# Two MLPs behind linear attention: the first MLP's block 0 split out of PSUM in turns 2 to 5, the left outputs moved to the sums' bank, three of its products placed among the last turns

## The chip, the cores and the metric

One core of a Trainium2 chip runs the whole kernel. Its engines are PE (TensorE), DVE (VectorE), ACT (ScalarE), POOL (GpSimd) and SP, which issues most DMAs. The metric is the device time of one execution in microseconds.

## What is computed

```python
def phi(x):
    proj = np.einsum('bhsd,df->bhsf', x, w_phi)
    proj = proj - np.max(np.abs(proj), axis=-1, keepdims=True)
    return np.concatenate([np.exp(proj), np.exp(-proj)], axis=-1)
q_p, k_p = phi(q), phi(k)                       # batch 4, heads 8, seq 576, head_dim 64, 128 features
kv, z = einsum('bhsf,bhsd->bhfd', k_p, v), k_p.sum(axis=2)
x = einsum('bhsf,bhfd->bhsd', q_p, kv) / (einsum('bhsf,bhf->bhs', q_p, z)[..., None] + 1e-06)
x = x.transpose(0, 2, 1, 3).reshape(2304, 512)
h = x @ w_in1;  x = np.maximum(0.01 * h, h) @ w_out1            # first MLP, 512 -> 2048 -> 512
h = x @ w_in2;  x = (h * np.tanh(softplus(h))) @ w_out2          # second MLP
```

## The kernel before

All products are of f32 values that are each split into a high part (`fp32r`, rounded by a copy on ACT) and a low part (value minus high part, a subtraction on DVE, L79 to L81); `three` (L83) makes one product from three matmuls, high by high, low by high and high by low. So each operand costs one ACT copy and one DVE subtraction.

**Attention.** A pair is two heads of one batch, 16 pairs in all (`PAIRS`), four of them per batch. Of the 576 positions, 512 are the main part and 64 the left part; left parts of two pairs are handled together. `attention(n)` (L515) is one turn, and works on five pairs at once: it transposes pair n+2 (`transposes`, PE, then a split), takes the cast of its left queries (`q_left`, DVE L361), projects pair n+1 (`q_proj`, copied by ACT as `qd`; `k_proj` with a guard of two DVE steps, L365 and L366), takes the exponentials of pair n (`k_exp`, `kp` and `lp`, once per sign, L388; `qp`) and its sums (`kv`, PE, into the PSUM tile `kvp`; `kv_copy`), the outputs of pair n-1 (`nd`, PE L448 and L453, into `outs`, two banks) and the normalising (`normalise`, DVE L461 `den` to L464 `xn`; `x_left`, ACT L474) and transposing of pair n-2 (`x_t`). POOL makes the maximum over the features for the queries (L408), two reductions per pair, started by ACT's `qd` copies and used by `q_guard` (DVE L412). `start` does the first projections before turn 0, among them pair 0's and the transposes of pair 1.

`x_t` (L477) transposes `xn` into the bank `xt`, forms the left output with one product against `fold` (L484), whose result lies in the last 64 columns of `outs`, copies that to X (ACT, L485), and returns the copy of the main part to X (ACT, L487), which the turn issues later. X holds the tokens in four chunks of 128 features; the pair's place in its batch is the chunk. The first batch's pairs are 0 to 3.

**Weights.** `conv0` (L93) turns w_in and w_out of the first MLP from their 8-byte form into f32, one unit of 128 x 512 per turn from turn 1 on: DVE L134 and L136 at the turn's head, ACT L150, DVE L159 and L162 at its end. The first ten units are also split, in the following turn (`Conv.split`, ACT L215, DVE L216); the last five are stored.

**First MLP.** Tokens go in blocks; block 0 is the main part of batch 0. `window(0, ...)` (L571) splits one chunk of its input X at the end of each of turns 8 to 11. `moe(g)` (L718) issues the g-th product of w_in (`emit_h`, 12 matmuls into a bank of the ring `a`), the leaky step (`leaky`: ACT L654, DVE L657, ACT L658, DVE L661), and the product of w_out for g-2 (`emit_o`, into four banks of the ring `b`, which is laid over the released banks of the attention). `moe(0)` and `moe(1)` stand at the ends of turns 15 and 16, after the normalising of the pairs 14 and 15; the last `x_t` and then `moe(2)` and the rest follow. From `moe(2)` on, weights of block 0 are made at two units per g.

Each engine runs its instructions in the order in which the program issues them (the schedule is a manual one), and so does each DMA queue.

Of the kernel before, what the change touches and what calls it, by code (L numbers as in the profile page):

```python
# [23 lines left out]
def attention_two_mlps_kernel(  # L24
# [18 lines left out]
    KD = DM // P  # L43
# [207 lines left out]
    with tc.manual_schedule():  # L251
# [105 lines left out]
        def q_left(i):  # L357
            s, l = st[i], lf[i // 2]
            c = P + (i % 2) * LEFT
            for x in "hl":  # L360
                nc.vector.tensor_copy(out=s["q" + x][:, HM:HM + LEFT], in_=l[x][:, c:c + LEFT].bitcast(F32))  # L361
# [17 lines left out]
        def k_proj_left(i):  # L379
            l = lf[i // 2]  # L380
            l["kd"] = ap.tile([P, 2, F], F32, tag="kdl", name="kdl", bufs=1)
            t = bank("a")
            three(t[:, 0:2 * F], l["h"][:, 0:P], l["l"][:, 0:P], wbh, wbl)
            k_guard(t[:, 0:2 * F].rearrange("p (n f) -> p n f", f=F), 2, l["kd"])
# [6 lines left out]
        def q_proj(i, c):  # L391
            s = st[i]
            h, o = divmod(c, 2)
            if "qd" not in s:
                s["qd"] = ap.tile([P, 2, S], F32, tag="qd", name="qd")
                s["qm"] = ap.tile([P, 2, S], F32, tag="qm", name="qm", bufs=1)
            t = bank("a")
            n = HM + (h == o) * LEFT
            c0 = h * (HM + (1 - o) * LEFT)
            d0 = (1 - o) * (HM + h * LEFT)  # L400
            f = slice(o * F, (o + 1) * F)
            three(t[:, 0:n], wbh[:, f], wbl[:, f], s["qh"][:, c0:c0 + n], s["ql"][:, c0:c0 + n])
            nc.scalar.activation(out=s["qd"][:, h, d0:d0 + n], in_=t[:, 0:n], func=AF.Copy)  # L403
            half = s.setdefault("half", set())
            half.add(c)
            if {2 * h, 2 * h + 1} <= half:
                qd, qm = s["qd"][:, h, :], s["qm"][:, h, :]
                nc.gpsimd.partition_all_reduce(qm, qd, P, bass_isa.ReduceOp.absmax)  # L408
# [68 lines left out]
        def x_t(i):  # L477
            s = st[i]
            b, p = divmod(i, NP)
            t = pa.tile([P, 512], F32, tag="xt", name="xt")  # L480
            for j in range(NM):
                nc.tensor.transpose(out=t[:, j * P:(j + 1) * P], in_=s["xn"][:, j].rearrange("p h d -> p (h d)"), identity=ident)
            o = s["nd"][:, 1, MAIN - LEFT:MAIN]
            nc.tensor.matmul(out=o, lhsT=s["xl"].rearrange("p h d -> p (h d)"), rhs=fold, start=True, stop=True)  # L484
            nc.scalar.activation(out=X[:, p, C0 + b * LEFT:C0 + (b + 1) * LEFT], in_=o, func=AF.Copy)  # L485
            st[i] = None
            return lambda: nc.scalar.activation(out=X[:, p, b * MAIN:(b + 1) * MAIN], in_=t, func=AF.Copy)  # L487

        def k_exp(i, a):
# [5 lines left out]
        def start():  # L495

            transposes(0, "k")
            split(wbh, wbl, wbd.rearrange("p a f -> p (a f)"))
            transposes(0, "q")
            k_proj(0, 0)  # L500
            transposes(0, "l")
            q_left(0)
            q_proj(0, 1)
            q_proj(0, 2)
            k_proj(0, 1)
            q_proj(0, 0)
            q_proj(0, 3)
            k_proj_left(0)
            transposes(1, "q", "k")
            q_left(1)  # L510
            q_guard(0)
            load(2)
            conv0.load(1)

        def attention(n):  # L515

            x, o, w, p, t = (i if 0 <= i < PAIRS else None for i in range(n - 2, n + 3))
            x_copy = lambda: None  # L520
            if n + 3 < PAIRS:
                load(n + 3)
            if t is not None and t > 1:
                values(t)
            if n >= CONV0:
                conv0.begin()
                conv0.split()
            if p is not None:
                for c in range(4):
                    q_proj(p, c)  # L530
            if x is not None and n < PAIRS:
                normalise(x)
                x_left(x)
            if p is not None:
                for c in range(2):
                    k_proj(p, c)
                if p % 2 == 0:
                    k_proj_left(p)
            if w is not None:
                k_exp(w, 0)  # L540
            if x is not None:
                x_copy = x_t(x)
            if t is not None:
                transposes(t)
                q_left(t)
            if w is not None:
                k_exp(w, 1)
            x_copy()
            conv0.scale()
            if o is not None:  # L550
                nd(o)
            if p is not None:
                q_guard(p)
            conv0.join()
            if w is not None:
                st[w]["qp"] = [exp(st[w]["qd"], "qp", sg) for sg in (1, -1)]
                for a in range(2):
                    kv(w, a)
                kv_copy(w)
            if p is None:  # L560
                normalise(o)
                x_left(o)
            if p is None:
                moe(n - PAIRS + 1)

        order = [(0, MAIN), (MAIN, MAIN), (C0, B * LEFT)] + [(j * MAIN, MAIN) for j in range(2, B)]
        blocks = [(a, c0, n) for a in range(2) for c0, n in order]
        NB = len(blocks)
        win = {}

        def window(j, chunks=range(KD)):  # L571
            a, c0, n = blocks[j]
            for kk in chunks:
                hi = winp.tile([P, MAIN], F32R, tag="wh", name="wh")[:, 0:n]
                lo = winp.tile([P, MAIN], F32R, tag="wl", name="wl")[:, 0:n]
                split(hi, lo, X[:, kk, c0:c0 + n])
                win.setdefault(j, []).append((hi, lo))


# [138 lines left out]
        def moe(g):  # L718
            for x in [g, g + 1] if g == jump else [g + 1] if g > jump else [g]:
                if x < len(seq):  # L720
                    emit_h(seq[x])
                    if seq[x][1][-1] == M - 1 and seq[x][0] + 1 < NB:
                        window(seq[x][0] + 1)
            if g < len(seq):
                j, ms = seq[g]
                if j <= last1:
                    between = leaky(seq[g])
                    if j == 0 and ms[0] >= HEAD:
                        conv1.step(*between)
                        if not conv1.done():  # L730
                            conv1.step()
                        if conv1.at == len(conv1.units):
                            conv2.load(1)
                    else:
                        for f in between:
                            f()
            if 0 <= g - 2 < len(seq) and seq[g - 2][0] <= last1:
                j, ms = seq[g - 2]
                emit_o(seq[g - 2])
                if ms[-1] == M - 1:  # L740
                    for d in range(KD):
                        finish(j, d)
                if 0 < j < last1:
                    conv2.step()
                    if conv2.done() and not w_st:
                        load_w2(0)
                if j == last1:
                    m = ms[0]
                    split_w2(m, (0, 1) if m < M - 1 else (0,))
                    if m < M - 1:  # L750
                        load_w2(m + 1, (0, 1) if m < M - 2 else (0,))
                    else:
                        load_w2(m, (1,))
                        tail[0] = g + 1
            if g == tail[0]:
                split_w2(M - 1, (1,))
            done = None
            if 0 <= g - 3 < len(seq) and seq[g - 3][0] > last1:
                j, ms = seq[g - 3]
                if seq[g - 3] == seq[-1]:  # L760

                    emit_o(seq[-1], (0, 1))
                    finish(j, 0)
                    finish(j, 1)
                    for d in (2, 3):
                        for it in seq[-2:]:
                            emit_o(it, (d,))
                        finish(j, d)
                elif seq[g - 3] == seq[-2]:
                    emit_o(seq[-2], (0, 1))  # L770
                else:
                    emit_o(seq[g - 3])
                    if ms[-1] == M - 1:
                        done = j
            mish(g, done)

        start()
        for n in range(PAIRS + 1):
            attention(n)
            if 0 <= n - PAIRS // 2 < KD:  # L780
                window(0, (n - PAIRS // 2,))
        x_t(PAIRS - 1)()
        ap.release()
        pa.release()
# [44 lines left out]
```

## Time and profile before

| what | value |
|---|---|
| time, median of 3 runs | 981.86 us (980.54 to 982.08) |
| time of the profiled execution | 982.12 us |
| its span, on the core | 980.0 us |
| PE busy | 957.1 us, 98% |
| DVE, ACT, POOL busy | 715.9, 507.2, 69.0 us |
| chain that ended last | PE 83%, DVE 7%, ACT 7% |

The span is the time on the core from the first instruction to the last; the execution's own time is some 2.1 us longer. The attention takes about the first 190 us of the span, the two MLPs the rest. A time in a row counts from the span's start. In the timeline, a bracket behind an instruction is how long its engine stood idle before it, and what released it.

### The profile page before, as it was taken

What the parts mean: (1) busy time and instruction counts of PE and PEld (TensorE: products, weight loads), DVE (VectorE), ACT (ScalarE), POOL (GpSimd) and SP (SyncE); (2) the same over time, 40 slices, a digit from 0 to 9 for tenths busy, and PEclk for the clock granted to TensorE, in tenths of its full rate; (3) what the DMA queues carried; (4) which work ended last, traced back from release to release, by engine and by line L of the source; (5) the groups of instructions that cost most, each with busy time, mean ns of one, the idle gap of its engine ahead of it and who ended that gap; (6) DMA issues with size and microseconds to landing.
All of it is one profiled execution on the core that took longest, in us unless ns stands there. A gap on an engine that the chain in (4) does not pass through costs nothing.

```text
span 980.0 us, 16741 instructions
## 1 busy us (share of the span) xinstructions
PE 957.1 (98%) x6704; PEld 818.4 (84%) x6704; DVE 715.9 (73%) x1271; ACT 507.2 (52%) x886; POOL 69.0 (7%) x36
## 2 busy tenths in 40 slices
PE   7999889899999999999999999999999999999998
PEld 7999778788888889988888888888888988888886
DVE  7899889389936665765334459878977788778875
ACT  5899879555523333333333456445545455445543
POOL 3443434000000000000000000000000000000000
PEclk9999999999999999999999999999999999999999
DMA  7444543235404444442203310001000100001001
GB/s 200 123 130 136 141 112 108 77 115 161 134 22 143 148 142 148 131 147 100 76 1 112 104 55 11 1 1 43 1 1 1 43 1 23 1 0 43 1 1 43
DMA packets 68205, 72.97 MB, mean 74 GB/s; under 512 B 27168, under 2 KB 52640, under 8 KB 68128
## 3 DMA queue, kind: packets, MB, share of 16 engines
q1 hardware_dynamic: 67392, 71.52, 23.8%
q8 instruction: 52, 0.85, 0.4%
q10 hardware_dynamic: 736, 0.39, 0.1%
q14 instruction: 25, 0.20, 0.1%
HBM read 57.48 MB, written 14.42 MB: 73 GB/s over the span
## 4 chain that ended last, share of the span: by engine, by line
PE 83%; DVE 7%; ACT 7%; issue 1%; DMA 0%; POOL 0%; POOLq 0%; ACTq 0%; DVEq 0%
PE a L84 14%; PE a L85 14%; PE a L86 14%; PE b L86 13%; PE b L85 13%; PE b L84 13%; ACT kp L388 2%; ACT qp L388 1%; DVE wl L216 1%; DVE xn L464 1%; DVE mx L365 1%; PE outs L448 1%; DVE qd L412 1%; DVE kd L366 1%; ACT xleft L474 1%
## 5 line engine op out<-in xcount | busy, mean ns | idle before, releaser
L84 PE MATMUL a<-wh,wh 128*128 128x512 f32 (+1 forms) x640 | 235.7, 368 | 0.0
L86 PE MATMUL a<-wh,wl 128*128 128x512 f32 (+1 forms) x640 | 235.4, 368 | 0.0
L85 PE MATMUL a<-wl,wh 128*128 128x512 f32 (+1 forms) x640 | 235.4, 368 | 0.0
L84 PEld LDWEIGHTS a<-wh,wh 128*128 128x128 f32 x640 | 120.6, 188 | 20.4 <-issue 0.2
L85 PEld LDWEIGHTS a<-wl,wh 128*128 128x128 f32 x640 | 120.7, 189 | 20.3
L86 PEld LDWEIGHTS a<-wh,wl 128*128 128x128 f32 x640 | 120.6, 188 | 19.9
L661 DVE TENSOR_TENSOR gl<-g,gh 128x512 fp32r<-128x512 f32 x72 | 49.8, 692 | 110.2 <-ACT gh L658 110.2
L85 PE MATMUL b<-gl,wh 128*128 128x512 f32 (+1 forms) x320 | 117.7, 368 | 0.0
L84 PE MATMUL b<-gh,wh 128*128 128x512 f32 (+1 forms) x320 | 117.7, 368 | 0.0
L86 PE MATMUL b<-gh,wl 128*128 128x512 f32 (+1 forms) x320 | 117.7, 368 | 0.0
L86 PE MATMUL b<-wh,gl 128*128 128x512 f32 x288 | 112.2, 390 | 0.0
L85 PE MATMUL b<-wl,gh 128*128 128x512 f32 x288 | 112.2, 389 | 0.0
L84 PE MATMUL b<-wh,gh 128*128 128x512 f32 x288 | 112.1, 389 | 0.0
L658 ACT ACTIVATE gh<-g 128x512 fp32r<-128x512 f32 x72 | 45.5, 632 | 116.0 <-PE b L86 110.7
L683 ACT ACTIVATE gh<-u 128x512 fp32r<-128x512 f32 x72 | 45.5, 633 | 70.3 <-PE b L85 63.6
L657 DVE TENSOR_TENSOR g<-g,a 128x512 f32<-128x512 f32 x72 | 49.4, 686 | 41.1 <-ACT g L654 38.4
L408 POOL PARTITION_ALL_REDUCE qm<-qd x32 | 68.8, 2197 | 100.7 <-ACT qd L403 94.0
L710 ACT ACTIVATE r<-e,two 128x512 f32<-128x512 f32 x72 | 51.7, 718 | 36.5 <-DVE e L695 36.5
L84 PEld LDWEIGHTS b<-gh,wh 128*128 128x128 f32 x320 | 60.4, 189 | 10.1
L86 PEld LDWEIGHTS b<-gh,wl 128*128 128x128 f32 x320 | 60.3, 189 | 10.0
L85 PEld LDWEIGHTS b<-gl,wh 128*128 128x128 f32 x320 | 60.3, 188 | 9.9
L679 ACT ACTIVATE e<-a 128x512 f32<-128x512 f32 x72 | 43.0, 597 | 47.8 <-PE a L86 26.8
(116 smaller groups left out, 1638.2 us busy)
## 6 DMA issues: line engine op xcount, KB each, us to landing
stage<-in_moe_w_in_dram SPq DMA_DIRECT2D x32, 512.0 KB, 3.8
stage<-in_moe_w_out_dram SPq DMA_DIRECT2D x32, 512.0 KB, 3.6
scr<-c SPq DMA_DIRECT2D x37, 256.0 KB, 2.0
wstage<-scr SPq DMA_DIRECT2D x32, 256.0 KB, 3.7
qn<-in_q_dram SPq DMA_DIRECT2D x16, 256.0 KB, 4.6
vmain<-in_v_dram SPq DMA_DIRECT2D x32, 128.0 KB, 3.4
kn<-in_k_dram SPq DMA_DIRECT2D x15, 256.0 KB, 4.4
out_dram<-X SPq DMA_DIRECT2D x15, 256.0 KB, 2.1
```

Of the source, the lines that this page charges most:

```text
L84: nc.tensor.matmul(out=o, lhsT=wh_, rhs=xh, start=start, stop=False)
L85: nc.tensor.matmul(out=o, lhsT=wh_, rhs=xl, start=False, stop=False)
L86: nc.tensor.matmul(out=o, lhsT=wl_, rhs=xh, start=False, stop=stop)
L216: return lambda: nc.vector.tensor_tensor(out=lo, in0=src, in1=hi.bitcast(F32), op=ALU.subtract)
L388: nc.scalar.activation(out=e, in_=src, func=AF.Exp, scale=float(sg))
L408: nc.gpsimd.partition_all_reduce(qm, qd, P, bass_isa.ReduceOp.absmax)
L657: nc.vector.tensor_tensor(out=g, in0=g, in1=h, op=ALU.max)
L658: nc.scalar.activation(out=hi, in_=g, func=AF.Copy)
L661: nc.vector.tensor_tensor(out=lo, in0=g, in1=hi.bitcast(F32), op=ALU.subtract)
L679: nc.scalar.activation(out=e0, in_=h0, func=AF.Exp)
L683: nc.scalar.activation(out=hi2, in_=u2, func=AF.Copy)
L710: nc.scalar.activation(out=r0, in_=e0, func=AF.Ln, bias=two)
```

## The change

- `x_t` of the pairs of batch 0 (turns 2 to 5) no longer returns the copy of `xt` to X: it returns `window(0, (p,), t)`, which splits the chunk straight out of the PSUM bank `xt` (ACT high part, DVE low part). The calls of `window(0, ...)` at the ends of turns 8 to 11 are gone.
- The left output's product goes to the last 64 columns of the next pair's `kvp` tile instead of `outs`. That tile holds one bank and is the one that the next `kv` will write.
- In `start`, pair 1's q transposes and its left casts come before the left keys' projection, the k transposes after it. In turn 0, the second exponential of the keys comes before the transposes of pair 2.
- In turn 15 the second exponential comes first, then `moe(0)`, then `x_t`; `moe(1)` comes at the end of turn 15; `emit_h` of the third product comes ahead of the last `x_t`, and `moe` leaves it out.

```diff
--- before.py
+++ after.py
@@ -480,10 +480,13 @@
             t = pa.tile([P, 512], F32, tag="xt", name="xt")
             for j in range(NM):
                 nc.tensor.transpose(out=t[:, j * P:(j + 1) * P], in_=s["xn"][:, j].rearrange("p h d -> p (h d)"), identity=ident)
-            o = s["nd"][:, 1, MAIN - LEFT:MAIN]
+            o = st[min(i + 1, PAIRS - 1)]["kvp"][:, MAIN - LEFT:MAIN]
             nc.tensor.matmul(out=o, lhsT=s["xl"].rearrange("p h d -> p (h d)"), rhs=fold, start=True, stop=True)
             nc.scalar.activation(out=X[:, p, C0 + b * LEFT:C0 + (b + 1) * LEFT], in_=o, func=AF.Copy)
-            st[i] = None
+            if i < PAIRS - 1:
+                st[i] = None
+            if b == 0:
+                return lambda: window(0, (p,), t)
             return lambda: nc.scalar.activation(out=X[:, p, b * MAIN:(b + 1) * MAIN], in_=t, func=AF.Copy)
 
         def k_exp(i, a):
@@ -505,9 +508,10 @@
             k_proj(0, 1)
             q_proj(0, 0)
             q_proj(0, 3)
+            transposes(1, "q")
+            q_left(1)
             k_proj_left(0)
-            transposes(1, "q", "k")
-            q_left(1)
+            transposes(1, "k")
             q_guard(0)
             load(2)
             conv0.load(1)
@@ -538,12 +542,17 @@
                     k_proj_left(p)
             if w is not None:
                 k_exp(w, 0)
+            if n == 0:
+                k_exp(w, 1)
+            if n == PAIRS - 1:
+                k_exp(w, 1)
+                moe(0)
             if x is not None:
                 x_copy = x_t(x)
             if t is not None:
                 transposes(t)
                 q_left(t)
-            if w is not None:
+            if w is not None and 0 < n < PAIRS - 1:
                 k_exp(w, 1)
             x_copy()
             conv0.scale()
@@ -560,20 +569,20 @@
             if p is None:
                 normalise(o)
                 x_left(o)
-            if p is None:
-                moe(n - PAIRS + 1)
+            if n == PAIRS - 1:
+                moe(1)
 
         order = [(0, MAIN), (MAIN, MAIN), (C0, B * LEFT)] + [(j * MAIN, MAIN) for j in range(2, B)]
         blocks = [(a, c0, n) for a in range(2) for c0, n in order]
         NB = len(blocks)
         win = {}
 
-        def window(j, chunks=range(KD)):
+        def window(j, chunks=range(KD), src=None):
             a, c0, n = blocks[j]
             for kk in chunks:
                 hi = winp.tile([P, MAIN], F32R, tag="wh", name="wh")[:, 0:n]
                 lo = winp.tile([P, MAIN], F32R, tag="wl", name="wl")[:, 0:n]
-                split(hi, lo, X[:, kk, c0:c0 + n])
+                split(hi, lo, X[:, kk, c0:c0 + n] if src is None else src)
                 win.setdefault(j, []).append((hi, lo))
 
 
@@ -718,7 +727,8 @@
         def moe(g):
             for x in [g, g + 1] if g == jump else [g + 1] if g > jump else [g]:
                 if x < len(seq):
-                    emit_h(seq[x])
+                    if x != HEAD:
+                        emit_h(seq[x])
                     if seq[x][1][-1] == M - 1 and seq[x][0] + 1 < NB:
                         window(seq[x][0] + 1)
             if g < len(seq):
@@ -777,8 +787,7 @@
         start()
         for n in range(PAIRS + 1):
             attention(n)
-            if 0 <= n - PAIRS // 2 < KD:
-                window(0, (n - PAIRS // 2,))
+        emit_h(seq[HEAD])
         x_t(PAIRS - 1)()
         ap.release()
         pa.release()
```

In `start`, on DVE, around the casts of pair 1's left queries (`qth`, `qtl` from `lh`, `ll`); `kd` is pair 0's guard, `mx` and `kdl` that of the left keys:

```order
 L366 TENSOR_TENSOR kd<-a,mx 128x512
+L81 TENSOR_TENSOR qtl<-a,qth 128x2x256
+L361 CAST qth<-lh 128x64
+L361 CAST qtl<-ll 128x64
 L365 TENSOR_REDUCE mx<-a 128x2
 L366 TENSOR_TENSOR kdl<-a,mx 128x256
-L81 TENSOR_TENSOR qtl<-a,qth 128x2x256
-L81 TENSOR_TENSOR ktl<-a,kth 128x512
-L361 CAST qth<-lh 128x64
-L361 CAST qtl<-ll 128x64
+L81 TENSOR_TENSOR ktl<-a,kth 128x512
```

The q subtraction and both casts stand ahead of the left keys' guard now, and the k subtraction behind it.

On DVE in turn 2, between the casts of pair 4 and `q_guard` (L412); `wl` is the low part of block 0's first chunk:

```order
 L361 CAST qth<-lh 128x64
 L361 CAST qtl<-ll 128x64
+L81 TENSOR_TENSOR wl<-xt,wh 128x512
 L412 TENSOR_TENSOR qd<-qd,qm 128x1152
 L159 SCALAR_TENSOR_TENSOR e<-stage 128x512
```

The subtraction that read X at the end of turn 8 reads the bank `xt` here; the same is found in turns 3, 4 and 5, and the four of turns 8 to 11 are gone.

On PE in turns 14 and 15, from the sums of pair 14 (`kvp` from `vmain`, `kp`) to the first product of the first MLP (`a` from `wh`):

```order
 L425 MATMUL kvp<-vmain_104,kp 64x65 x16
 L428 MATMUL kvp<-vleft_107,lp 64x2x65 x2
-L482 MATMUL xt<-ident,xn 128x128 x4
-L484 MATMUL outs<-fold,xleft_86 128x64
-L448 MATMUL outs<-kv,qp 64x65 x32
-L453 MATMUL outs<-kv,qp 64x65 x4
-L425 MATMUL kvp<-vmain_102,kp 64x65 x16
-L428 MATMUL kvp<-vleft_105,lp 64x2x65 x2
-L425 MATMUL kvp<-vmain_102,kp 64x65 x16
-L428 MATMUL kvp<-vleft_105,lp 64x2x65 x2
 L84 MATMUL a<-wh,wh_597 128x512
 L85 MATMUL a<-wl,wh_597 128x512
```

The first MLP's product follows the sums of pair 14 at once; the transposes of pair 13, the outputs of pair 14 and the sums of pair 15 come after its twelve matmuls.

## Rows read from the trace of the kernel before

**Rows 1.** Page, first part: busy time, share of the span, instructions, by engine

```profile
PE 957.1 (98%) x6704; PEld 818.4 (84%) x6704; DVE 715.9 (73%) x1271; ACT 507.2 (52%) x886; POOL 69.0 (7%) x36
```

**Rows 2.** Windows: busy us (instructions) of each engine, granted clock, DMA share, GB/s

```profile
178.00:180.00 2.00, 2.00 (x43) 2.00 (x42) 0.69 (x1) 0.40 (x1) 0.00 (x0) 0.50 0.02 7
200.00:220.00 20.00, 20.00 (x90) 16.56 (x89) 19.12 (x36) 10.96 (x20) 0.00 (x0) 1.00 0.39 130
```

**Rows 3.** Timeline of DVE, start; start us, us, instruction, idle before and its releaser

```profile
14.02 0.88 DVE L361 CAST qth<-lh 128x64 fp32r<-128x64 f32 x1
14.82 0.18 DVE L361 CAST qtl<-ll 128x64 fp32r<-128x64 f32 x1
15.78 1.36 DVE L412 TENSOR_TENSOR qd<-qd,qm 128x1152 f32<-128x1152 f32 x1 [0.78 <-POOL qm L408]
18.66 0.69 DVE L365 TENSOR_REDUCE mx<-a 128x4 f32<-128x512 f32 x1 [1.52 <-PE a L86]
...
23.05 1.35 DVE L412 TENSOR_TENSOR qd<-qd,qm 128x1152 f32<-128x1152 f32 x1
...
26.94 0.69 DVE L365 TENSOR_REDUCE mx<-a 128x4 f32<-128x512 f32 x1 [1.87 <-PE a L86]
```

**Rows 4.** Timeline of PE, start

```profile
15.05 0.38 PE L84 MATMUL a<-qth,wbh 128*128 128x320 f32 x1 [2.51 <-DVE qtl L361]
...
23.01 1.16 PE L425 MATMUL kvp<-vmain,kp 128*64 128x65 f32 x32 [0.79 <-ACT kp L388]
...
24.32 0.41 PE L84 MATMUL a<-qth,wbh 128*128 128x320 f32 x1
```

**Rows 5.** Timeline of POOL, two reductions in a row of it

```profile
11.44 4.31 POOL L408 PARTITION_ALL_REDUCE qm<-qd  x2 [11.01 <-ACT qd L403]
...
66.91 4.26 POOL L408 PARTITION_ALL_REDUCE qm<-qd  x2 [6.23 <-ACT qd L403]
...
108.28 4.31 POOL L408 PARTITION_ALL_REDUCE qm<-qd  x2 [6.74 <-ACT qd L403]
```

**Rows 6.** Timeline of DVE, turns 6 to 12

```profile
76.80 0.16 DVE L461 TENSOR_SCALAR den<-outs 128x10 f32<-128x10 f32 x1
...
97.23 0.16 DVE L461 TENSOR_SCALAR den<-outs 128x10 f32<-128x10 f32 x1
...
107.10 0.69 DVE L81 TENSOR_TENSOR wl<-X,wh 128x512 fp32r<-128x512 f32 x1 [1.43 <-ACT wh L80]
...
108.38 1.78 DVE L216 TENSOR_TENSOR wl<-c,wh 128x512 fp32r<-128x512 f32 x1
...
146.30 0.16 DVE L461 TENSOR_SCALAR den<-outs 128x10 f32<-128x10 f32 x1
```

**Rows 7.** Timeline of all engines, end of turn 4

```profile
62.07 1.35 DVE L412 TENSOR_TENSOR qd<-qd,qm 128x1152 f32<-128x1152 f32 x1
62.18 0.62 ACT L487 ACTIVATE X<-xt 128x512 f32<-128x512 f32 x1
...
66.25 0.69 DVE L216 TENSOR_TENSOR wl<-c,wh 128x512 fp32r<-128x512 f32 x1 [0.75 <-ACT wh L215]
```

**Rows 8.** Timeline of PE, turns 14 to 16

```profile
168.68 2.09 PE L448 MATMUL outs<-kv,qp 128*64 128x65 f32 x64 [0.73 <-ACT X L485]
...
174.59 0.63 PE L482 MATMUL xt<-ident,xn 128*128 128x128 f32 x4 [1.27 <-DVE xn L464]
...
176.50 3.66 PE L448 MATMUL outs<-kv,qp 128*64 128x65 f32 x64 [0.90 <-ACT X L485]
...
187.85 2.09 PE L448 MATMUL outs<-kv,qp 128*64 128x65 f32 x64 [1.57 <-ACT X L485]
```

**Rows 9.** Timeline of ACT, turns 15 and 16

```profile
177.29 0.59 ACT L487 ACTIVATE X<-xt 128x512 f32<-128x512 f32 x1
...
185.70 0.60 ACT L654 ACTIVATE g<-a 128x512 f32<-128x512 f32 x1 [1.99 <-PE a L86]
...
187.59 0.20 ACT L485 ACTIVATE X<-outs 128x64 f32<-128x64 f32 x1
```

## The prediction

> **What bounds the kernel now.** I read three views, in this order. The page's first part [rows 1] shows PE busy 957.1 of 980.0 us, so only some 23 us of the span can be had without taking matmuls away. The windows [rows 2] say where: in 200 to 220 us, as in all the MLP stretches after it, PE is busy 20.00 of 20.00 at a granted clock of 1.00, while DVE is busy 19.12; in 178 to 180 it is also always busy, but at a granted clock of 0.50, the lower of its two levels (1.2 GHz). So the losses lie ahead of the MLPs, in the attention turns and their ends. The timelines tell what ends each wait: at the start PE waits for DVE and ACT [rows 3, 4]; in the sixteen turns DVE and ACT hand the work to each other and PE merely follows [rows 6, 7]; in the last turns PE waits again, for copies of ACT and for DVE [rows 8]. From PE's first product of the first MLP after the attention, all that follows is a fixed length of PE work. What the change is worth is therefore how much earlier PE gets there. Three places count.
>
> **Turns: the split taken out of turns 8 to 11.** A turn's head on DVE is the `den` row. From 76.80 to 97.23 are two plain turns (6 and 7): 20.43 us. From 97.23 to 146.30 are turns 8 to 11, each ending with `window`: 49.07 us [rows 6]. Four plain turns would be 40.86; turn 11 has no weight split behind it (L216, 0.69 in [rows 7]), so 40.2. The split of X costs 8.9 us there. The rows show why it costs more than its own 0.69: DVE waits 1.43 us for ACT's high half, and the weight split that follows takes 1.78 instead of 0.69, because it now starts at 108.38, just after POOL's reduction of 108.28 [rows 5, 6], where in a plain turn it is through when POOL starts (66.25 and 0.69 in [rows 7], POOL at 66.91 in [rows 5]). So 1.1 us of each is DVE held up by POOL.
>
> In turns 2 to 5 the same split comes back cheaper. ACT pays nothing: its copy of `xt` into X (0.62 [rows 7]) becomes the high half of the same size, and nothing reads X there before the MLP overwrites it. DVE gets one subtraction of 0.69 more. It stands ahead of `q_guard` and waits for ACT: in an even turn ACT's copy ends at 62.18 + 0.62 = 62.80, DVE was free at 62.07, so 0.73 of waiting and 0.69 of work, 1.42 in all; of this 0.75 was idle before L216 anyway [rows 7], which leaves 0.67. In an odd turn I count no such idle time and ACT's copy as done: 0.69. Four turns: 2.7 us. L216 moves later by 0.7, and so do ACT's `qd` copies that start POOL, so it stays ahead of POOL. Bounds: 4.2 (even turns pay all 1.42) and 1.4 (only odd turns pay). Net gain 8.9 - 2.7 = 6.2, between 8.2 - 4.2 = 4.0 and 8.9 - 1.4 = 7.5.
>
> **Start.** PE stands 2.51 us at 15.05 for the cast of pair 1's left queries, and the casts took 0.88 and 0.18 [rows 3, 4], the first one held up by POOL. The change puts the q transposes three matmuls earlier and the casts right behind the q subtraction; by ACT's 0.60 and DVE's 0.69 the casts run near 13.3, between the holds of POOL's two reductions (11.44 and 2.15 later [rows 5], 1.1 each as above). PE goes on some 1.6 us earlier. The next gate is `q_guard(0)` at 15.78, which waits for POOL and doesn't move; with its 1.36, of which some 0.1 overlaps the next, the guard of pair 1's keys starts at 17.05 and not at 18.66 after 1.52 idle [rows 3]. From there to the end of the casts DVE takes 23.05 - 18.66 = 4.39 [rows 3], to 21.44. In the present order PE starts pair 2's q products only at 24.32, behind the second half of the sums, which waited 0.79 for ACT's second exponential [rows 4]; in the new order both exponentials come before ACT's copies, so PE follows DVE at about 21.5. That is 2.8 earlier, and the guard of pair 2, at 26.94 after 1.87 idle for PE [rows 3], moves with it. I take 2.8. Bounds: 0.8 (only that 0.79 goes, the casts fall into a hold again) and 3.4 (both DVE waits, 1.52 + 1.87). The k transposes move behind the left keys; their DVE subtraction then ends near 14.9, when PE is still at pair 1's q products, so I cost it at nothing. DMA: nothing is added, and SP's issues keep their order.
>
> **Last turns.** PE waits 0.73 (168.68), 1.27 (174.59), 0.90 (176.50) and 1.57 (187.85): 4.47; three of these are `nd` waiting for ACT's copy out of `outs`, one is `x_t` waiting for `xn` [rows 8]. And `nd` takes 3.66 at 176.50 for a usual 2.09, at the lower granted clock [rows 2, 8]: 1.57 more. Together 6.0. With the left product in the `kvp` bank `nd` no longer waits for that copy; with 12 first-MLP matmuls ahead of `x_t(13)`, `x_t(14)` and `x_t(15)`, DVE's `xn` and ACT's scaling are covered each time. PE's idle stretch ahead of 176.5 is filled, so I take the clock to stay up. Two waits are new. First, `kv(15)` writes the `kvp` bank that ACT must first have read (L485), and ACT now has the first MLP's two steps ahead of that read: they would start at 177.29, and from L654 to L485 it is 187.59 - 185.70 = 1.89, so the read ends at 177.29 + 1.89 + 0.20 = 179.4 [rows 9]. PE, without the 0.73, 1.27 and 0.90 but with 2.8 of products, would be through `nd(14)` at about 178.2: a wait of 1.2; behind it in PE's queue stand all the rest. Second, the output banks of the MLP reuse the attention's banks, and the first product into them waits for ACT's last copies; the products that covered this now come before `x_t(15)`, so PE waits for copies of 0.20 and 0.59 [rows 9] and their start, 0.9. Gain 6.0 - 2.1 = 3.9. Bounds: 6.0 (neither wait) and 2.3 (both, and the low clock as now).
>
> Elsewhere, in turns 6 to 14, the new bank does nothing: PE's `nd` starts a little earlier, but PE is not what the turn waits for.
>
> **The sum.** 2.8 + 6.2 + 3.9 = 12.9. The profiled execution took 982.12 us (span 980.0 and 2.1 around it), 0.26 above the median 981.86 of the runs; 982.1 - 12.9 = 969.2. By the bounds, one term at a time, 967.1 to 971.4. The case around the sum has a chance of 0.60. A measurement of this kernel can tell about 0.2% (2 us) from no change.
>
> **Rivals.** *The start keeps its pace*: the casts fall into POOL's hold, or the clock drops as PE's idle times shift. For it: the margin of the casts to the second hold is some 0.3 us. Start 0.8, so 971.2; chance 0.15.
> *The last turns only trade waits*: `kv(15)` waits, and the clock falls in that gap as it did before 178. Against it: single gaps of 1.27 in [rows 8] came together with 0.90 before the fall. Tail 2.3, so 970.8; chance 0.12.
> *The weight split meets POOL in turns 3 to 6*: the moved split pushes L216 behind POOL's start, as it did after turn 8. 4 x 1.1 = 4.4 more, 973.6. Against it: whatever delays L216 also delays the `qd` copies that start POOL; the margin is POOL's start at 66.91 against L216's at 66.25. Chance 0.07. The rows show DVE held for 1.1 us of a reduction of about 2.15 [rows 5, 6]. The Trainium skill (SBUF — State Buffer, Who interferes with whom) states that the two engines share a port pair as an exclusive lock, and that whoever comes second is blocked for the other's whole instruction. By that rule a collision would cost up to about 2.1 us and this rival 975 or more (an estimate); the trace disagrees on the length, and the measured 1.1 decides.
> *Slower*: the shared `kvp` bank ties PE to ACT in every turn. `kv` of turns 2 to 15 may only start when ACT has read the left product of the same turn. The copy ended at about 168.66, and `nd` of 2.09 lies between [rows 8]; with `nd` starting 0.73 earlier the slack is 1.4. If ACT's copy came later than this by d in each of 14 turns, PE's next products, ACT's `qd` copies and POOL would follow: 14 d. It overtakes the 12.9 from d = 0.92; at d = 1.1 it costs 15.4, so 984.6. Against it: the copy's place in ACT's order is unchanged. Chance 0.04. That the gains cancel within 2 us has 0.02.
>
> **How the numbers follow.** Faster holds the first four cases, 0.94. The forecast is the sum's case, 969.2. The range takes in the first three (0.87): its top is 971.2 with 0.8 for the spread of runs (980.54 to 982.08) and 0.5 for small misses in the other terms, 972.5; its low end is 967.3, where start and turns both reach their upper bounds (0.6 + 1.3 less), with 0.8 for that spread and 0.5 as above, 966.0.
>
> **What would show it.** Right: DVE `wl<-xt` in four early turns, turns 2 to 5 about 0.7 longer, turns 8 to 11 like 6 and 7 with every L216 near 0.69; pair 2's q products on PE near 21.5; no PE wait for `xn` in the last turns, one of about 1 us before `kv(15)` and one before the first `b` product. Wrong: L216 rows of 1.8 in turns 3 to 6; the early DVE waits for PE unchanged; a stretch at granted clock 0.50 near 180; or PE waits appearing after 200 us, where DVE is nearly full [rows 2].

## The result and the profile after

The changed kernel took 967.82 us (median of 4 runs, 967.59 to 968.7), the kernel before 981.2 us beside it (4 runs, 980.42 to 982.08): ratio 0.9865, interval 0.9848 to 0.9882, so 13.4 us less. Measured once more at the end, it took 968.77 against 981.15 (ratio 0.987, 0.9856 to 0.9884), 12.4 us less. The forecast was 969.2, with 966.0 to 972.5.

Its profiled execution took 967.76 us, with a span of 965.9. This table cuts both spans at the same instructions: POOL's first reduction, the `den` rows on DVE that head the turns, and PE's first product into the banks `b`. Each length is the difference of two starts. The stretch from the head of turn 15 to the first `b` product is called the tail below.

| stretch | before | after | gain | forecast |
|---|---|---|---|---|
| up to POOL's first reduction | 11.44 | 10.66 | 0.78 | none |
| from there to the head of turn 2 | 24.49 | 21.81 | 2.68 | 2.8 |
| turns 2 to 5 | 40.87 | 43.33 | -2.46 | -2.7 |
| turns 6 and 7 | 20.43 | 20.44 | 0 | 0 |
| turns 8 to 11 | 49.07 | 40.18 | 8.89 | 8.9 |
| turns 12 to 14 | 27.00 | 27.02 | 0 | 0 |
| head of turn 15 to the first `b` product | 23.08 | 18.75 | 4.33 | 3.9 |
| from there to the end of the span | 783.6 | 783.7 | -0.1 | 0 |

**Busy time.** The page's first part, against [rows 1]:

```profile
PE 950.6 (98%) x6704; PEld 813.9 (84%) x6704; DVE 711.6 (74%) x1271; ACT 505.2 (52%) x882; POOL 68.5 (7%) x36
```

ACT has 4 instructions fewer: the four copies of `xt` to X became the high halves, and the four high halves of turns 8 to 11 are gone. PE's matmuls are the same in number. The windows of the last turns and of the MLP, against [rows 2]:

```profile
175.00:180.00 5.00, 5.00 (x88) 4.47 (x87) 2.46 (x5) 2.44 (x6) 0.00 (x0) 1.00 0.53 188
200.00:220.00 20.00, 20.00 (x90) 16.57 (x89) 19.08 (x35) 10.59 (x19) 0.00 (x0) 1.00 0.52 155
```

The stretch at 0.50 is gone, and the MLP is as full as it was.

**Start.** The timeline of DVE, against [rows 3]:

```profile
12.29 0.56 DVE L361 CAST qth<-lh 128x64 fp32r<-128x64 f32 x1
12.39 0.49 DVE L361 CAST qtl<-ll 128x64 fp32r<-128x64 f32 x1
...
14.96 1.36 DVE L412 TENSOR_TENSOR qd<-qd,qm 128x1152 f32<-128x1152 f32 x1 [0.99 <-POOL qm L408]
16.24 0.68 DVE L365 TENSOR_REDUCE mx<-a 128x4 f32<-128x512 f32 x1
...
20.79 1.36 DVE L412 TENSOR_TENSOR qd<-qd,qm 128x1152 f32<-128x1152 f32 x1
...
23.55 0.69 DVE L365 TENSOR_REDUCE mx<-a 128x4 f32<-128x512 f32 x1 [0.72 <-PE a L86]
```

The casts are through at 12.88, as POOL's second reduction begins (10.66 + 2.13 = 12.79), the guard of pair 1's keys (16.24) follows `q_guard(0)` without its 1.52 of idle time, and that of pair 2 waits 0.72 instead of 1.87.

**Turns.** The timeline of all engines in turn 4, against [rows 7] and POOL's 66.91 in [rows 5], and then that of DVE at the heads of turns 6, 8 and 12, against [rows 6]:

```profile
60.60 0.69 DVE L81 TENSOR_TENSOR wl<-xt,wh 128x512 fp32r<-128x512 f32 x1 [0.67 <-ACT wh L80]
61.21 1.35 DVE L412 TENSOR_TENSOR qd<-qd,qm 128x1152 f32<-128x1152 f32 x1
...
64.65 0.69 DVE L216 TENSOR_TENSOR wl<-c,wh 128x512 fp32r<-128x512 f32 x1
...
65.31 2.14 POOL L408 PARTITION_ALL_REDUCE qm<-qd  x1 [6.86 <-ACT qd L403]
```

```profile
75.80 0.16 DVE L461 TENSOR_SCALAR den<-outs 128x10 f32<-128x10 f32 x1
...
96.24 0.16 DVE L461 TENSOR_SCALAR den<-outs 128x10 f32<-128x10 f32 x1
...
136.42 0.16 DVE L461 TENSOR_SCALAR den<-outs 128x10 f32<-128x10 f32 x1
```

DVE's new subtraction waits 0.67 for ACT in an even turn; the weight split (L216) lost its 0.75 of idle time and starts 0.66 before POOL, as it did before (66.25 and 66.91).

**Last turns.** The timeline of PE, against [rows 8], and that of ACT in turn 15, against [rows 9]:

```profile
166.12 2.09 PE L448 MATMUL outs<-kv,qp 128*64 128x65 f32 x64
...
169.46 1.15 PE L425 MATMUL kvp<-vmain,kp 128*64 128x65 f32 x32 [1.02 <-ACT X L485]
...
174.80 0.60 PE L482 MATMUL xt<-ident,xn 128*128 128x128 f32 x4
...
175.49 2.09 PE L448 MATMUL outs<-kv,qp 128*64 128x65 f32 x64
...
182.19 0.50 PE L84 MATMUL b<-gh,wh 128*128 128x512 f32 x1 [0.80 <-ACT X L490]
```

```profile
167.31 0.60 ACT L663 ACTIVATE g<-a 128x512 f32<-128x512 f32 x1
168.66 0.63 ACT L667 ACTIVATE gh<-g 128x512 fp32r<-128x512 f32 x1 [0.76 <-DVE g L666]
169.20 0.21 ACT L485 ACTIVATE X<-kvp 128x64 f32<-128x64 f32 x1
```

`nd` and `x_t` start with no wait and at the upper clock. `kv(15)` waits for ACT's read of the left product, which stands behind two steps of the first MLP on ACT.

### The profile page after: what moved, and what is told of

Same layout as the page of the kernel before. It is cut to its first block, busy times and chain, and to the rows that moved or that the text cites. A ratio compares the mean times of both kernels' runs of the same rounds, so it can differ in the third digit from the quotient of the medians.

```text
span 965.9 us, 16740 instructions
## 1 busy us (share of the span) xinstructions
PE 950.6 (98%) x6704; PEld 813.9 (84%) x6704; DVE 711.6 (74%) x1271; ACT 505.2 (52%) x882; POOL 68.5 (7%) x36
## 4 chain that ended last, share of the span: by engine, by line
PE 85%; DVE 9%; ACT 5%; POOL 1%; issue 1%; DMA 0%; POOLq 0%; ACTq 0%; DVEq 0%
PE a L84 14%; PE a L85 14%; PE a L86 14%; PE b L84 14%; PE b L86 14%; PE b L85 14%; DVE qd L412 1%; DVE mx L365 1%; ACT kp L388 1%; DVE kd L366 1%; DVE xn L464 1%; POOL qm L408 1%; ACT qp L388 1%; DVE wl L216 1%; PE outs L448 1%; PE kvp L425 1%
```

## The experiments

The table has the stretches of the profiles, cut as above, and the medians. The kernel before took 981.02 us beside the first four experiments, 981.33 beside the next four and 981.15 beside the last four. Turns 6 and 7 take 20.43 to 20.45 and turns 12 to 14 27.00 to 27.02 in every profile.

| kernel | POOL first | to turn 2 | turns 2 to 5 | turns 8 to 11 | turn 15 to `b` | median (lowest to highest) |
|---|---|---|---|---|---|---|
| before | 11.44 | 24.49 | 40.87 | 49.07 | 23.08 | 981.2 |
| after | 10.66 | 21.81 | 43.33 | 40.18 | 18.75 | 967.82 |
| e_turns | 12.23 | 23.89 | 43.32 | 40.14 | 21.49 | 974.65 (973.32 to 975.35) |
| e_start | 10.65 | 21.79 | 40.88 | 49.76 | 21.49 | 978.76 (977.36 to 979.66) |
| e_kvp | 11.47 | 24.47 | 40.88 | 49.06 | 18.88 | 978.87 (976.77 to 980.64) |
| e_tail | 11.77 | 23.25 | 40.88 | 49.09 | 18.73 | 978.36 (976.65 to 979.44) |
| e_outs | 11.69 | 21.78 | 43.32 | 40.16 | 24.05 | 974.1 (974.07 to 974.54) |
| e_place | 11.47 | 24.47 | 40.87 | 45.19 | 23.08 | 977.75 (975.89 to 978.25) |
| e_lo | 10.68 | 23.80 | 42.05 | 40.16 | 18.74 | 968.25 (966.4 to 968.81) |
| e_last | 10.64 | 21.77 | 43.35 | 40.16 | 16.80 | 966.71 (965.93 to 967.3) |
| after_again | 11.20 | 21.78 | 43.33 | 40.15 | 18.76 | 968.77 (967.71 to 969.61) |
| e_casts | 12.08 | 21.77 | 43.31 | 40.14 | 18.74 | 968.52 (967.86 to 969.22) |
| e_both | 11.33 | 21.78 | 42.07 | 40.15 | 16.80 | 965.94 (964.73 to 966.49) |
| e_best | 10.56 | 21.83 | 42.05 | 40.15 | 16.81 | 965.64 (964.64 to 966.17) |

**One part of the change alone** (edits to the kernel before; the diffs are pieces of the change's). `e_turns` has the split out of `xt` and no `window(0, ...)` in turns 8 to 11:

> Only the split of block 0 is moved to turns 2 to 5; start, left outputs and last turns as before. Theory (three gains that add up): turns 2 to 5 each about 0.6 us longer than before's 10.5 and 9.9, turns 8 to 11 together 40.2 instead of 49.07, all L216 rows near 0.69; net 6.4 us less, about 975 where before takes 981. The waits of the last turns stay (0.73, 1.27, 0.90, 1.57) with the stretch at granted clock 0.50. Rival (the gain needs the earlier start or the shared bank): L216 still meets POOL in turns 3 to 6 or the gain stays under 4 us.

Ratio 0.9938 (0.992 to 0.9956). Turns 2 to 5 pay 2.45 and turns 8 to 11 save 8.93, as in the whole change. `e_start` has the new order in `start` and turn 0:

> Only the order in the start and in turn 0 is changed. Theory: q_guard of pair 2 (31.85 before) comes 2.7 us earlier relative to POOL's first reduction (11.44 before), and the whole 2.7 us earlier. Rival (what was seen at the start was the first microseconds of another execution): relative to POOL's first reduction under 1 us is left, and the time is as before.

Ratio 0.9978 (0.9967 to 0.9988). The start is 2.70 shorter, as in the whole change. (Its turn 10 ran partly at a granted clock of 0.50, and turns 8 to 11 took 0.7 longer than before's.) `e_kvp` has the left product in the `kvp` bank:

> Only the left outputs move to the kvp bank. Theory: the three waits of nd for ACT's copy go; x_t(13) still waits for xn, so the 0.73 of turn 14 is lost to that wait; 0.90 + 1.57 and perhaps 0.2 stay as gain: 2.5 to 2.9 us if the stretch at granted clock 0.50 stays, 4.1 to 4.5 if it goes. The turns up to 13 keep their heads to 0.1 us. Rival (the last turns gain by the products that fill them): under 1 us, as other waits take the place.

Ratio 0.998 (0.9968 to 0.9991). `e_tail` adds the early first-MLP products to that:

> The left outputs in the kvp bank and the three first-MLP products among the last turns; start and split of block 0 as before. Theory: heads of turns 2 to 14 as before, then 4.3 us gained up to the first product of w_out: waits of about 1.0 before kv(15) and 0.8 before that product, none for xn, no stretch at granted clock 0.50 near 176 to 180. Rival (the clock stays up only because the whole is shifted): the stretch at 0.50 remains and the gain is about 2.7.

Ratio 0.9976 (0.9966 to 0.9986). With the bank alone the profile's tail is 4.20 shorter, and the products add 0.15. In `e_kvp` PE's timeline has one wait left, larger than before:

```profile
174.63 0.63 PE L482 MATMUL xt<-ident,xn 128*128 128x128 f32 x4 [2.09 <-DVE xn L464]
```

The products fill this 2.09 and pay with two new waits, 1.02 and 0.80 in the changed kernel: 0.27 of net gain, of which 0.15 shows. And a caution: `e_turns` and `e_start` leave the last turns as they were, with the same waits, and yet their tail is 1.59 shorter than before's, because the low clock, expected to stay in `e_turns`, did not come (in `e_place`, with the same last turns again, it did: 23.08). PE's timeline of `e_turns`, at the place of 176.50 in [rows 8]:

```profile
168.33 0.63 PE L482 MATMUL xt<-ident,xn 128*128 128x128 f32 x4 [1.26 <-DVE xn L464]
...
170.25 2.09 PE L448 MATMUL outs<-kv,qp 128*64 128x65 f32 x64 [0.89 <-ACT X L485]
```

Waits of 1.26 and 0.89 here, of 1.27 and 0.90 before, and 2.09 against 3.66 for the same matmuls. So of the tail's 4.33 about 1.6 belongs to a fall of the clock that the tail's waits alone do not decide.

The mean granted clock, which is on record for every run beside the experiments and every run of the changed kernels, says how often stretches at the low clock came. The kernel before ran 41 times beside the experiments: 35 times at 0.996 to 0.998, in 980.26 to 983.18 us, and six times at 0.999, in 978.27 to 979.62. The changed kernel had 0.999 or 1.000 in all of its eight runs. With one part of the change alone the mean was 0.998 or less in 3 of 4 runs of `e_turns`, in all ten of `e_start` and of `e_kvp`, and in 8 of 10 of `e_tail`. So the whole change kept the clock up each time, and no part alone did so; where in an unprofiled run the clock was low, and which parts it takes to keep it up, is not shown. Against before's six runs at 0.999 (median 979.5) the changed kernel's eight (median 968.2) are 11.3 us faster.

**The bank undone in the whole change** (`e_outs`).

```diff
-            o = st[min(i + 1, PAIRS - 1)]["kvp"][:, MAIN - LEFT:MAIN]
+            o = s["nd"][:, 1, MAIN - LEFT:MAIN]
```

> The changed kernel with one part undone: the left product goes back into the bank of the main sums (outs); the early split, the start and the early first-MLP products stay. Theory (the two parts of the tail need each other: nd waits for ACT's copy out of outs, and with the first MLP's ACT steps ahead of that copy it waits longer): PE's wait for kvp (1.0) goes, PE's waits for outs come back, about 0.7 in turn 14, about 3 before nd(14) and about 1.6 before nd(15); first b product 3 to 4 us later than in the changed kernel's profile (182.19), so 971 to 972 us. Rival (the early products alone cover the waits, the bank is worth nothing): first b product within 1 us of the changed kernel's, 967 to 969 us. Heads of turns 2 to 12 as in the changed kernel under both, but for the start's own 1 to 2 us.

The ratio to before is 0.9927 (0.9912 to 0.9942): 5.3 to 6.3 us slower than the two measurements of the changed kernel. The tail is 5.30 longer. PE's timeline, and the window behind the largest wait:

```profile
159.77 2.09 PE L448 MATMUL outs<-kv,qp 128*64 128x65 f32 x64 [0.73 <-ACT X L485]
...
170.40 3.61 PE L448 MATMUL outs<-kv,qp 128*64 128x65 f32 x64 [2.44 <-ACT X L485]
...
181.75 2.09 PE L448 MATMUL outs<-kv,qp 128*64 128x65 f32 x64 [1.57 <-ACT X L485]
```

```profile
172.00:174.00 2.00, 2.00 (x42) 2.00 (x40) 0.36 (x1) 0.00 (x0) 0.00 (x0) 0.50 0.41 135
```

0.73 + 2.44 + 1.57 = 4.74 of waits, 1.52 at the low clock (3.61 against 2.09), less the 1.02 for `kvp` that is gone: 5.24. The waits came where the theory had them; its 3 to 4 us were too small by the clock. Without the bank the early products are a loss: 24.05 against before's 23.08, both with a stretch at the low clock. That stretch followed a wait of 2.44 here, and all four runs had a mean granted clock of 0.998.

**The split left late, but put elsewhere in the turn** (`e_place`, an edit to the kernel before).

```diff
             x_copy()
+            if 0 <= n - PAIRS // 2 < KD:
+                window(0, (n - PAIRS // 2,))
             conv0.scale()
...
             attention(n)
-            if 0 <= n - PAIRS // 2 < KD:
-                window(0, (n - PAIRS // 2,))
```

> The kernel before with one edit: the split of X in turns 8 to 11 stays there and still reads X in SBUF, but is written ahead of conv0.scale, nd and q_guard instead of at the turn's end. Theory (the price of the late split is its place: DVE waits 1.4 us for ACT there, and the weight split behind it meets POOL): no L216 of 1.8 us, turns 8 to 11 take 43 to 44.5 us from head to head instead of 49.07, time 976 to 977 us, most of what moving the split to turns 2 to 5 gives (974.65 us). Rival (it needs the read from PSUM in place of ACT's copy, because ACT then has one more instruction of 0.6 in these turns): turns 8 to 11 take 47 us or more, time 979 us or more.

Ratio 0.9957 (0.994 to 0.9973). The timelines of ACT and of DVE in turn 8:

```profile
103.05 0.62 ACT L487 ACTIVATE X<-xt 128x512 f32<-128x512 f32 x1
103.53 0.66 ACT L80 ACTIVATE wh<-X 128x512 fp32r<-128x512 f32 x1
```

```profile
104.22 0.69 DVE L81 TENSOR_TENSOR wl<-X,wh 128x512 fp32r<-128x512 f32 x1 [1.19 <-ACT wh L80]
...
108.28 0.69 DVE L216 TENSOR_TENSOR wl<-c,wh 128x512 fp32r<-128x512 f32 x1
```

No L216 is held by POOL any more, and 3.88 of the 8.89 comes from the place alone. The rest, 45.19 against 40.18, stays: 1.15, 0.81, 1.15 and 1.91 over the plain turns 8 to 11. In turn 8 the rows say what it is: ACT's high half stands behind its copy of `xt` to X, so DVE waits 1.19 for it and then works 0.6, while the 0.75 of idle time that L216 has in a plain turn is gone, 1.05 in all. That is the rival's additional ACT instruction. Turn 11 ends with no L216, and there POOL catches another DVE step (L136, 1.52 instead of 0.42), in this kernel as before. The truth lies between theory and rival: neither's range has 45.19, or the median of 977.75.

**The low part behind the guard** (`e_lo`, an edit to the changed kernel: in turns 2 to 5 the subtraction is issued after `q_guard`).

```diff
             if p is not None:
                 q_guard(p)
+            for lo, src, hi in late:
+                nc.vector.tensor_tensor(out=lo, in0=src, in1=hi.bitcast(F32), op=ALU.subtract)
+            late.clear()
```

> The changed kernel with DVE's low part of the early split (turns 2 to 5) issued behind q_guard instead of ahead of it; ACT's high part stays. Theory (the 0.67 us that DVE waits for ACT in each even turn is on the path, the guard can run in it): turns 2 to 5 cost about 0.6 to 1.4 us together over plain ones instead of 2.45, time 0.8 to 1.4 us under the changed kernel's 967.8, so 966.4 to 967.0; L216 stays at 0.69. Rival (something else ends the turn, as q_guard then waits for PE, or the weight split now meets POOL): turns 2 to 5 within 0.4 of the changed kernel's or longer by up to 4.4, time 967.4 to 972.

Ratio 0.9863 (0.9848 to 0.9878). Turns 2 to 5 are 1.28 shorter, the subtraction never waits, as expected; but the median did not move, as under the rival. What its profiled execution lost lies in the start, which this edit does not touch. PE, then DVE:

```profile
10.76 0.63 PE L341 MATMUL a<-ident,qn 128*128 128x128 f32 x4 [0.21 <-DMA qn<-in_q_dram]
```

```profile
12.10 0.69 DVE L81 TENSOR_TENSOR qtl<-a,qth 128x512 fp32r<-128x512 f32 x1 [1.22 <-ACT qth L80]
12.71 0.18 DVE L361 CAST qth<-lh 128x64 fp32r<-128x64 f32 x1
12.81 1.33 DVE L361 CAST qtl<-ll 128x64 fp32r<-128x64 f32 x1
...
18.41 0.69 DVE L365 TENSOR_REDUCE mx<-a 128x4 f32<-128x512 f32 x1 [1.61 <-PE a L86]
```

PE's transposes of pair 1's queries waited for their load and started 0.39 us later than in the changed kernel's profile (10.37); the second cast met POOL's second reduction (10.68 + 2.13 = 12.81) and took 1.33, and PE went on at a granted clock of 0.50 between 16 and 18 us. The head of turn 2 came 23.80 behind POOL's first reduction instead of 21.8. That is the prediction's rival "the start keeps its pace", in one execution, the run of 968.81 with a mean granted clock of 0.998. The other three had 0.999 or 1.000 and took 966.4, 967.95 and 968.56; why two of them gained nothing is not shown.

**The two new waits in the last turns** (`e_last`, an edit to the changed kernel).

```diff
             if n == PAIRS - 1:
                 k_exp(w, 1)
-                moe(0)
+                emit_h(seq[0])
             if x is not None:
                 x_copy = x_t(x)
+            if n == PAIRS - 1:
+                moe(0)
...
-        emit_h(seq[HEAD])
-        x_t(PAIRS - 1)()
+        emit_h(seq[HEAD], range(KD - 1))
+        x_last = x_t(PAIRS - 1)
+        emit_h(seq[HEAD], (KD - 1,))
+        x_last()
```

> The changed kernel with two edits in the last turns: in turn 15 ACT's copy of the left product comes ahead of the first MLP's first ACT steps, and of the last first-MLP product the fourth chunk comes behind the last x_t instead of ahead of it. Theory (kv(15) waits 1.02 for ACT's read of the kvp bank because two ACT steps of the MLP stand ahead of it, and the first b product waits 0.80 because its cover has gone ahead): both waits fall, the first to 0 and the second to 0.2 or less; first b product 1.3 to 1.7 us earlier, time 966.1 to 966.5. Rival (the waits only hide others, x_t then waits for xn or the first b product for the leaky steps): first b product within 0.4 us of the changed kernel's, 967.4 to 968.2.

Ratio 0.985 (0.9835 to 0.9865); the tail is 1.95 shorter, more than expected (the median, 966.71, is 0.2 above the expected range), and PE's timeline has no wait in it, down to the first `b` product:

```profile
168.22 1.10 PE L425 MATMUL kvp<-vmain,kp 128*64 128x65 f32 x32
...
180.18 0.50 PE L84 MATMUL b<-gh,wh 128*128 128x512 f32 x1
```

Both waits were on the path, with their whole 1.82.

**The casts ahead of the transposes, and all together.** `e_casts` puts the casts of pair 1's left queries ahead of its q transposes; `after_again` is the changed kernel; `e_both` is `e_lo` with `e_last`; `e_best` adds the casts' new place.

```diff
+            parts_of(1, "q", HM + LEFT)
+            q_left(1)
             transposes(1, "q")
-            q_left(1)
```

> The changed kernel itself once more, beside the next three on the same chip. Theory (the start hangs on whether pair 1's left casts get through before POOL's second reduction, which differs between executions): median 967.5 to 968.5; in the profile the head of turn 2 comes either 21.8 us behind POOL's first reduction, with casts of 0.5, or 23.8, with a cast of 1.3. Rival (the late start seen once belongs to another cause, as a late load): some other row ahead of the casts is longer.

> The changed kernel with one edit in the start: the casts of pair 1's left queries come ahead of its q transposes and of the subtraction that waits for ACT, not behind them. Theory (the casts' place is a margin of some 0.3 us before POOL's second reduction): the casts take 0.2 each and end before POOL's second reduction starts, no cast of over 0.5; head of turn 2 at 21.3 to 21.9 us behind POOL's first reduction in every profile; median 0 to 1 us under the changed kernel's of the same call, and a narrower spread. Rival (the casts write the tile that PE still reads for pair 0, so they wait and hold back the q subtraction): head of turn 2 more than 22.2 us behind, median 0.3 or more above.

> The changed kernel with the low parts of the early split behind q_guard (measured alone: turns 2 to 5 1.28 us shorter) and the two edits in the last turns (measured alone: first b product 2.0 us earlier). Theory (they lie in different places and add): 3.3 us under the changed kernel of the same call, less 1 to 2 in executions whose start is late: 964.3 to 966. Rival (they share ACT or the clock, or the weight split of a later turn moves): less than 2 us under it.

> The kernel before this one with the start's casts ahead of the q transposes too: three edits to the changed kernel. Theory: as the last, and its start never late: 3.3 to 4.3 us under the changed kernel of the same call, 963.8 to 965, with a narrower spread. Rival (the casts hold back the q subtraction): no better than the last, 964.3 to 966.

`after_again` showed the first of its two expected starts, 21.78 with casts of 0.56 and 0.50; its median lies 0.3 above the range given for it. `e_casts` was no better (968.52 and 968.77, with spreads of 1.4 and 1.9). The expectation that the casts would take 0.2 fell: they now meet POOL's first reduction. DVE and POOL in `e_best`:

```profile
10.68 1.23 DVE L369 CAST qth<-lh 128x64 fp32r<-128x64 f32 x1
11.82 0.18 DVE L369 CAST qtl<-ll 128x64 fp32r<-128x64 f32 x1
```

```profile
10.56 4.31 POOL L416 PARTITION_ALL_REDUCE qm<-qd  x2 [10.13 <-ACT qd L411]
```

It costs nothing, since `q_guard(0)` still waits for POOL (0.92 in `e_best`, 0.86 in `e_casts`): the head of turn 2 comes 21.83 and 21.77 behind POOL's first reduction, as where the casts pass between the reductions. So 21.8 is set by POOL, and the late start of `e_lo` was not met in these two profiles. Whether the new place removes it can't be told from one profile each. `e_both` is 2.83 under `after_again` in the medians, with 3.2 in the stretches (1.26 in the turns, 1.96 in the tail): they add. `e_best`, 965.64 us, ratio 0.9838 (0.9824 to 0.9851), has the lowest median here, but not measurably under `e_both`: the theory's 963.8 to 965 was missed, and its rival's range holds it.

## Why the prediction was right

*Turns.* 8.89 for 8.9 and 2.46 for 2.7. The working held step by step: the 0.67 of waiting in even turns (0.73 forecast), about 0.6 more in each turn, L216 ahead of POOL with no idle time left before it, and all 32 `wl<-c,wh` rows between 682 and 695 ns. In `e_place` 1.2 went with the place of the late split in each of turns 8, 9 and 10, near the 1.1 at which the prediction priced POOL's hold; in turn 11, where the hold stayed with another step in it, only 0.2.

*Start.* 2.68 for 2.8. With the 0.78 by which POOL began earlier taken off, the rows lie where the sum put them: the guard of pair 1's keys at 16.24 + 0.78 = 17.02 (17.05), PE's q products of pair 2 at 20.95 + 0.78 = 21.73 (21.5). But part of this is luck. `e_tail` and `e_turns`, which have the old start, needed 23.25 and 23.89 and not 24.49, at a granted clock of 1.00 where before had 0.55 and 0.60 in 16 to 20 us. The windows of before and of `e_tail`, and DVE's casts in `e_turns`:

```profile
16.00:18.00 2.00, 2.00 (x12) 2.00 (x11) 1.14 (x1) 1.51 (x5) 0.69 (x1) 0.55 1.04 369
```

```profile
16.00:18.00 2.00, 2.00 (x18) 2.00 (x17) 1.39 (x2) 1.85 (x6) 0.43 (x2) 1.00 1.06 389
```

```profile
14.81 0.88 DVE L361 CAST qth<-lh 128x64 fp32r<-128x64 f32 x1
15.61 0.92 DVE L361 CAST qtl<-ll 128x64 fp32r<-128x64 f32 x1
```

DVE's wait for PE ahead of the guard of pair 1's keys, 1.52 before, was 0.50 in `e_tail` and 1.18 in `e_turns`. In `e_turns` POOL held both casts, in `e_tail` and before only the first. So against executions without that low clock the new order is worth 1.5 to 2.1, and 2.7 against one with it.

*Tail.* 4.33 for 3.9, with both new waits near their forecast: 1.02 for 1.2 and 0.80 for 0.9. (By the prediction's own terms, 176.50 - 2.90 + 2.8 + 2.09, PE would have arrived at 178.5 and not 178.2, and the first wait would be 0.9.) The waits went as it said: no `nd` waits for ACT, and no `x_t` for `xn`. What it did not see is how little the 12 matmuls ahead of each `x_t` add: run alone, the bank gives nearly the whole gain, and the products give back in new waits what they cover. The 1.57 of low clock was counted as the change's because PE's idle stretch is filled. That reason is not shown: the stretch also vanished in `e_turns` and `e_start`, where the tail's waits stayed. The count itself held, with a mean granted clock of 0.999 or more in all eight runs of the changed kernel.

*The rivals.* "The last turns only trade waits" was right on the waits of the products and wrong on the sum. "L216 meets POOL" and "`kvp` ties PE to ACT in every turn" did not come: turns 12 to 14 kept 27.02, and PE waited for that bank once, in turn 15. "The start keeps its pace" came in one profile (`e_lo`) of the seven that have the change's start.

*The forecast's 1.4 us.* 0.78 is POOL's earlier start in this execution, which is chance, 0.4 the tail, and 0.2 the time around the span (1.9 for 2.1). By the separate runs the parts give 6.4 (`e_turns`), 2.3 (`e_start`) and 2.7 (`e_tail`), 11.3 in all, against 12.4 and 13.4 for the whole; with intervals of 1 to 2 us on each, they do not differ. The agreement is no proof that the parts are independent, for the low clock came more often in their runs than in the changed kernel's.

## What to carry to other kernels

Where an added step stands in its engine's queue can cost as much as the step: 3.9 of the 8.9 us of the late split went when only its place was changed, 3.3 of them (three times 1.1) because a DVE step behind it no longer fell just behind POOL's start. Before an engine gets other work to cover a wait, look at what stands behind that work in the other engines' queues; the early products covered 2.09 us and put ACT's read of a bank back by 1.02, and one small copy put first won that back. And measure a part both alone and taken out of the whole: the bank was worth 2.2 us alone (981.02 to 978.87) and 5.3 to 6.3 among the other parts, where its absence brought a stretch at the low clock too.

## What the runs showed of the hardware

- POOL's reduction holds a DVE step between SBUF tiles for about 1.2 us from its start: the 0.18 cast took 1.33 from 12.81 in `e_lo` and 1.23 in `e_best`. Up to its end it can hold again: in the changed kernel casts at 20.42 and 20.52 took 0.39 and 0.33, to 20.8, where the reduction ends (16.50 + 4.26 = 20.76), and in `e_turns` a cast at 15.61 took 0.92, to 16.53, with a reduction from 14.36 to 16.49. What opens the time between the two holds is not shown: a cast just as far into a reduction took 0.18 before (14.82 [rows 3], with a reduction from 13.59). The Trainium skill (SBUF — State Buffer, Who interferes with whom) has the loser blocked for the whole instruction, which would be 2.13; no step here was held so long.
- PE's first products run at one of two rates while the granted clock of the windows reads 1.00: 128x256 in 0.41 or in 0.28. The profiles of the changed kernel and of `e_casts` near 7 us, in that order:

```profile
6.99 0.28 PE L85 MATMUL a<-wbl,kth 128*128 128x256 f32 x1
```

```profile
7.27 0.41 PE L85 MATMUL a<-wbl,kth 128*128 128x256 f32 x1
```

The starts of such products lie 0.12 and 0.21 us apart, which for 256 columns is near the upper and the lower of the two levels (2.4 and 1.2 GHz). The faster rate comes at 5.8 us in the first profile and at 10.7 in the second, and POOL's first reduction follows at 10.66 and 12.08. In the 14 profiles it starts 10.56 to 10.68 where the faster rate had come by 6.8 us, 11.20 where it came near 8.4, and 11.33 to 12.23 where it came after 9: up to 1.7 us apart, more than many edits are worth. The Trainium skill (TensorE: Matmul & The Clock Gate, Part 1: The HAM clock gate) has PE begin at its lower level, be raised later, and the point differ from run to run; these rows agree, but the windows' granted clock does not show it there.
- The granted clock fell to its lower level (0.50) behind PE waits of 2.51 in before's start, of 1.27 and 0.90 in its tail, of 2.44 in `e_outs` and of 1.62 in turn 10 of `e_start`, and did not fall behind equal waits in `e_tail` and `e_turns` (2.51 at the start), in `e_turns` and `e_start` (tail) and in before's turn 10 (1.63). One such stretch costs 0.7 to 1.6 us, so one profile can't tell whose it is; the mean granted clock of many runs can tell how often it comes.
